# A decode layer on one core: a weight load moved behind the last value tile, batch rows 8 partitions apart for a single output store, and the last weight chunk in rows 6, 2, 1

## The chip, the cores and the metric

The kernel runs on 1 core of one Trainium2 chip. The metric is the device time of one execution in microseconds (us). The time before was 382.03 us, the median of 3 runs (381.35 to 382.17). In the runs that have both numbers the time is 1.7 to 2.2 us longer than the span of the profile (for instance 381.64 us and a span of 379.8 us; one run of before has 383.11 and 380.1 us), so times are compared with times and spans with spans.

## The reference, cut to what matters

One token of a transformer layer for a batch of 4, in bf16. The last 4096 positions of the K and V caches are used.

```python
# D = 576, 32 query heads, 16 KV heads, head size 128, F = 4608
x = A_x                                              # (4, 1, 576)
q = layernorm(x) @ wq                                # 32 heads
p = softmax(q . k_cache[last 4096] * 128 ** -0.5)
o = p . v_cache[last 4096]
h = x + o @ wo
n = layernorm(h)
out = h + (relu(n @ W_gate) * (n @ W_up)) @ W_down   # (4, 1, 576)
```

K and V make 134 MB of the 159.6 MB that must be read from HBM; wq, wo, W_gate, W_up and W_down are the rest. Almost nothing is written.

## The kernel before

All bulk loads are issued in one fixed order by SyncE, into one region of SBUF, `arena`. Each load first waits until the readers of the bytes that it overwrites are done. `add_kv` puts a tile of 4 MB into one of four slots. wo needs 18432 elements a partition: the 16384 where the widened queries lay, and the first 2048 of slot 0, where V12 lies. So wo waits for PV12, the product that reads V12.

```python
        WO_OFF = 0
        for g in range(NTILE - 4, NTILE):            # V12, V13, V14, V15
            if g == NTILE - 1:
                place(("wo",), WO_OFF, H * D, "WO",
                      lambda e: e.dma_start(out=arena[:, WO_OFF:WO_OFF + H * D], in_=A_wo.rearrange("(p r) n -> p (r n)", p=128)))
            add_kv("V", g)
        # ... W_gate and W_up ...
        for j in range(4):                           # W_down in four chunks of 9 rows a partition
            wd_off.append(off)
            for r0, r1 in ((0, 9),) if j < 3 else ((0, 6), (6, 9)):
                place(("wd", j, r0), off + r0 * D, (r1 - r0) * D, "DOWN", ...)
```

The end of the program: the down product takes 4 matmuls for each row (one for each quarter of the 576 output columns, in its own quadrant of 32 PSUM partitions), 144 in all. VectorE casts the result, and four stores of 4 rows bring it out.

```python
        for j in range(4):
            for r in range(9):
                for n in range(4):
                    deps = []
                    if n == 0 and (r == 0 or (j == 3 and r == 6)):
                        deps = [("L", "wd", j, r)] + (["HC0", "HC1", "HC2"] if j == 0 else [])
                    pe("DOWN", lambda e, ...: e.matmul(
                        bank[0][32 * n:32 * n + 32, 0:144], lhsT=hhT[:, r * 128 + 32 * j:r * 128 + 32 * j + 32],
                        rhs=wv[:, r, 144 * n:144 * (n + 1)], start=False, stop=(j == 3 and r == 8), ...), deps)
        dve("OUT", lambda e: e.tensor_copy(out=out_sb[:, :], in_=bank[0][:, 0:144]), ["DOWN"])
        orow = out.rearrange("b s d -> (b s) d")
        for n in range(4):
            P.dma("sync" if n % 2 == 0 else "scalar", ("O", n),
                  lambda e, n=n: e.dma_start(out=orow[:, 144 * n:144 * (n + 1)], in_=out_sb[32 * n:32 * n + 4, :]), f"d_out{n}", ["OUT"])
        P.op("sync", None, None, [("O", n) for n in range(4)])
```

The four batch rows lie on partitions 32n, 32n+1, 32n+2 and 32n+3 of each quadrant n.

## Time and profile before

| what | before |
|---|---|
| time | 382.03 us (381.35 to 382.17) |
| span of the profiled execution | 381.1 us |
| bytes read from HBM | 159.58 MB |
| PE, DVE busy | 73%, 59% of the span |

In the profiles PE is TensorE's matmuls, PEld its weight loads, DVE VectorE, ACT ScalarE, POOL GpSimd; SPq and ACTq are the issues of transfers by SyncE and ScalarE; PEclk is the share of TensorE's full clock that was granted.

From the page of before, the part in 40 slices: each digit is the busy share of a slice of 9.5 us in tenths, and the last line is what the transfer engines moved in GB/s.

```profile
PEclk9998999989978897798997887989989956756687
DMA  8999999999999999999999999999999999999993
GB/s 331 440 423 421 406 440 437 433 428 427 420 439 440 424 433 426 433 430 435 433 430 427 435 430 423 435 433 433 430 428 433 427 439 430 423 435 427 419 414 123
```

The transfer engines are busy 90% or more in all slices but the first and the last, and the windows from 300 to 360 us show a DMA share of 0.99 to 1.02. That is the limit: the weights and caches come in without a hole, and what can still be won lies behind their landing. So the end of the chain of waits, in order of time, is the place to read (start in us, length in us, what; the issues of W_down at 342.96 to 344.28 us and gaps of 0.04 us are left out):

```profile
309.94 3.63 PE psb L497 x32
313.59 0.34 SPq L271
313.97 25.30 DMA sb_arena<-in_A_v_cache_dram
339.31 3.63 PE psb L497 x32
344.28 33.27 DMA sb_arena<-in_B_W_down_dram
377.60 0.83 PE psb L701 x11
378.45 0.31 DVE sb_out_sb L704
```

PV12 ends, SyncE issues wo (L271), then V15 (L246), V15 lands 25.3 us later, PV15 runs, and the last W_down transfer is 33.27 us under way. A length of 33 us for 0.4 MB, which at the 430 GB/s of these slices is about 1 us of work (an estimate), says that the transfer stood in a queue: the wait before its issue isn't what bounds it. The timeline of before from 376 us on (start, length, engine, line, what; in brackets the idle time before and what ended it; here and below some lines of weight loads are left out):

```profile
376.55 1.86 PE L701 MATMUL psb<-sb_arena,sb_pp 128*32 128x144 bf16 x36 [1.31 <-DMA sb_arena<-in_B_W_down_dram]
377.60 0.13 PEld L701 LDWEIGHTS psb<-sb_arena,sb_pp 128*32 128x32 bf16 x6 [0.43 <-DMA sb_arena<-in_B_W_down_dram]
377.98 0.13 PEld L701 LDWEIGHTS psb<-sb_arena,sb_pp 128*32 128x32 bf16 x6 [0.25 <-issue]
378.45 0.31 DVE L704 CAST sb_out_sb<-psb 128x144 bf16<-128x144 f32 x1 [6.54 <-PE psb L701]
378.78 0.67 SPq L708 DMA_DIRECT2D out_dram<-sb_out_sb  x2
378.79 0.62 ACTq L708 DMA_DIRECT2D out_dram<-sb_out_sb  x2
```

The last three rows release PE at 377.60 us. Of their 12 weight loads six come at once and six at 377.98 us, after an idle time that the profile puts down to "issue".

### The profile page before, as it was taken

The numbers are of one execution on the slowest core, as the hardware profiler recorded it, in microseconds if no ns is written. First come the engines' busy times: TensorE is split into PE (matmuls) and PEld (weight loads), VectorE is DVE, ScalarE is ACT, GpSimd is POOL, SyncE is SP. The second block draws the span as 40 slices with busy tenths as digits, with TensorE's granted clock in tenths as the row PEclk, the third lists the DMA queues.
The fourth block names the chain that finished last, engine by engine and source line by source line (L and its number), as shares of the span: only waits on it lengthen the run. The fifth ranks groups of instructions, "written<-read, shape, count | busy, mean of one in ns | idle before, by whom it ended". The sixth has DMA issues, their size and how long they took to land.

```text
span 381.1 us, 3671 instructions
## 1 busy us (share of the span) xinstructions
PE 278.0 (73%) x1629; PEld 92.8 (24%) x1629; DVE 223.2 (59%) x157; ACT 37.5 (10%) x95; POOL 16.3 (4%) x38
## 2 busy tenths in 40 slices
PE   0057999989959892979996939899969537036544
PEld 0013223322222221222221212222212213015322
DVE  0796799979383917965828279756464455002210
ACT  1112000015000006000000051000000340000100
POOL 8800000000000000000000000000000000000000
PEclk9998999989978897798997887989989956756687
DMA  8999999999999999999999999999999999999993
GB/s 331 440 423 421 406 440 437 433 428 427 420 439 440 424 433 426 433 430 435 433 430 427 435 430 423 435 433 433 430 428 433 427 439 430 423 435 427 419 414 123
DMA packets 6390, 159.81 MB, mean 419 GB/s; under 512 B 740, under 2 KB 744, under 8 KB 1384
## 3 DMA queue, kind: packets, MB, share of 16 engines
q1 hardware_dynamic: 6352, 159.59, 97.7%
q8 instruction: 12, 0.20, 0.2%
q14 instruction: 2, 0.02, 0.0%
q10 hardware_dynamic: 24, 0.01, 0.0%
HBM read 159.58 MB, written 0.00 MB: 419 GB/s over the span
## 4 chain that ended last, share of the span: by engine, by line
PE 44%; DMA 34%; DVE 15%; POOL 2%; ACT 2%; issue 1%; SPq 0%; POOLq 0%
PE psb L450 38%; DMA sb_arena<-in_A_k_cache_dram 19%; DVE sb_arena L432 11%; DMA sb_arena<-in_B_W_down_dram 9%; DMA sb_arena<-in_A_v_cache_dram 7%; PE psb L497 5%; POOL sb_arena L303 2%; ACT sb_pp L475 2%; DVE sb_o_sel L509 1%; DVE sb_o_tmp L505 1%; DVE sb_pp L484 1%; PE psb L534 0%; ACT sb_arena L418 0%; SPq L286 0%; PE psb L469 0%
## 5 line engine op out<-in xcount | busy, mean ns | idle before, releaser
L450 PE MATMUL psb<-sb_arena 128*128 128x512 bf16 x512 | 209.1, 578 | 10.5 <-DVE sb_arena L432 8.2
L432 DVE STREAM_TRANSPOSE sb_arena<-sb_arena 128x4096 f32<-128x4096 f32 x32 | 156.1, 4901 | 48.5 <-DMA sb_arena<-in_A_k_cache_dram 48.4
L450 PEld LDWEIGHTS psb<-sb_arena 128*128 128x128 bf16 x512 | 56.8, 114 | 153.6 <-issue 130.3
L497 PE MATMUL psb<-sb_arena,sb_pp 128*32 128x512 bf16 x512 | 35.9, 431 | 23.0 <-DMA sb_arena<-in_A_v_cache_dram 16.5
L475 ACT ACTIVATE sb_pp<-psb,sb_stat 128x512 bf16<-128x512 f32 x32 | 24.9, 847 | 247.8 <-DVE sb_stat L470 247.8
L505 DVE TENSOR_TENSOR sb_o_tmp<-psb,sb_qm 128x512 f32<-128x512 f32 x16 | 10.8, 676 | 27.9 <-PE psb L497 27.9
L497 PEld LDWEIGHTS psb<-sb_arena,sb_pp 128*32 128x32 bf16 x512 | 13.6, 106 | 47.9 <-issue 22.7
L457 DVE TENSOR_REDUCE sb_stat<-psb 128x1 f32<-128x1024 f32 x4 | 4.8, 1211 | 24.2 <-PE psb L450 24.2
L484 DVE STREAM_TRANSPOSE sb_pp<-sb_pp 128x2048 bf16<-128x2048 bf16 x8 | 18.0, 2278 | 1.4 <-ACT sb_pp L475 1.4
L509 DVE TENSOR_REDUCE sb_o_sel<-sb_o_tmp 128x128 f32<-128x512 f32 x16 | 16.6, 1037 | 0.6
L534 PE MATMUL psb<-sb_o_sel,sb_selw 128*32 128x32 f32 x128 | 2.4, 232 | 16.3 <-DVE sb_o_sel L509 16.3
L668 PE MATMUL psb<-sb_arena,sb_hnT 128*32 128x384 bf16 x120 | 7.9, 437 | 6.6 <-DMA sb_arena<-in_B_W_up_dram 4.5
L375 PE MATMUL psb<-sb_ident_b,sb_xn_bf 4*128 4x4 bf16 x4 | 0.3, 172 | 13.7 <-DVE sb_xnd_bf L364 13.7
L388 PE MATMUL psb<-sb_arena,sb_xnT 128*32 128x512 bf16 x32 | 3.6, 631 | 8.9 <-DMA sb_arena<-in_A_wq_dram 8.9
L675 DVE TENSOR_TENSOR sb_pp<-psb,sb_pp 128x384 bf16<-128x384 f32 x3 | 1.5, 551 | 12.6 <-PE psb L668 12.6
L517 PE MATMUL psb<-sb_stat,sb_sameh 128*128 128x1 f32 x8 | 1.8, 292 | 9.1 <-DVE sb_stat L515 9.1
L303 POOL MEMSET sb_arena<- 128x8192 f32 x1 | 6.9, 6925 | 0.0
L475 ACT ACTIVATION_READ_ACCUMULATOR sb_pp<-psb,sb_stat 128x1 f32 x32 | 6.6, 208 | 0.0
L668 PEld LDWEIGHTS psb<-sb_arena,sb_hnT 128*32 128x32 bf16 x120 | 4.2, 124 | 9.7 <-DMA sb_arena<-in_B_W_up_dram 4.8
L534 PEld LDWEIGHTS psb<-sb_o_sel,sb_selw 128*32 128x32 f32 x128 | 1.9, 142 | 17.4 <-DVE sb_o_sel L509 17.4
L701 PE MATMUL psb<-sb_arena,sb_pp 128*32 128x144 bf16 x144 | 3.8, 250 | 3.0 <-DMA sb_arena<-in_B_W_down_dram 2.5
L418 ACT COPY sb_arena<-sb_q_keep 32x128 bf16<-32x128 bf16 x16 | 4.8, 303 | 1.5 <-DVE sb_q_keep L409 1.4
(123 smaller groups left out, 71.9 us busy)
## 6 DMA issues: line engine op xcount, KB each, us to landing
sb_arena<-in_A_k_cache_dram SPq DMA_DIRECT2D x16, 4096.0 KB, 18.9
sb_arena<-in_A_v_cache_dram SPq DMA_DIRECT2D x16, 4096.0 KB, 24.2
sb_arena<-in_A_wo_dram SPq DMA_DIRECT2D x1, 4608.0 KB, 16.0
sb_arena<-in_B_W_gate_dram SPq DMA_DIRECT2D x1, 4608.0 KB, 30.9
sb_arena<-in_B_W_up_dram SPq DMA_DIRECT2D x1, 4608.0 KB, 42.3
sb_arena<-in_A_wq_dram SPq DMA_DIRECT2D x1, 4096.0 KB, 21.5
sb_arena<-in_B_W_down_dram SPq DMA_DIRECT2D x3, 1296.0 KB, 31.1
sb_arena<-in_B_W_down_dram SPq DMA_DIRECT2D x1, 864.0 KB, 32.7
```

The lines of the kernel that those rows point to most:

```text
L303: pool("c_qW", lambda e: e.memset(arena[:, 0:2 * QWW].bitcast(FP32), 0.0))
L418: act(("QW", b), lambda e, i=i: e.copy(out=bass.AP(tensor=arena, offset=32 * i * AW + b % 2 * QWW + 32 * i, ap=[[AW, 32], [128, 4], [514, ...
L432: dve(("TRA", g, w), lambda e: e.transpose(out=dst, in_=src), [("L", "K", g)] if w == 0 else [])
L450: pe(("QK", g, w), lambda e, off=off, steps=steps, wo_=wo_, qd=qd, first=first, last=a == cb == 3: e.matmul(bank[SB[b % 2] + w], lhsT=aren ...
L457: dve(("MAX", b), lambda e: e.tensor_reduce(out=stat[:, b, 0:1], in_=s_ps, axis=AX.X, op=ALU.max, negate=True), [("QK", 4 * b + 3, 1)])
L475: act(("EXP", b, w), lambda e, w=w, a=a: e.activation(out=bass.AP(tensor=pp, offset=4096 + a // 2 * 2048 + w * 1024 + a % 2, ap=[[8192, 12 ...
L484: dve(("PTR", b, w), lambda e: e.transpose(out=dst, in_=src), [("EXP", b, w), ("PV", 4 * b - 1) if b else "QMM"])
L497: pe(("PV", g), lambda e, j=j, tq=tq, k=k: e.matmul(o_ps[32 * j:32 * j + 32, :], lhsT=pT[:, qd * 1024 + tq * 32:][:, 0:32], rhs=v[:, tq * ...
L505: dve(("OS", g), lambda e: e.tensor_tensor(out=o_tmp[:, :].rearrange("p (t d) -> p t d", t=4), in0=o_ps.rearrange("p (t d) -> p t d", t=4) ...
L509: dve(("OSEL", g), lambda e: e.tensor_reduce(out=o_sel[:, qd, :], in_=o_tmp[:, :].rearrange("p (t d) -> p d t", t=4), axis=AX.X, op=ALU.ad ...
L534: pe(("OT", b), lambda e, q=q, qd=qd: e.matmul(ot_ps[32 * qd:32 * qd + 32, 0:32], lhsT=selw[:, qd, 32 * q:32 * q + 32], rhs=o_sel[:, qd, 3 ...
L668: pe(("GU", g, c // 4), lambda e, g=g, m=m, j=j, lo=lo, c=c: e.matmul(bank[3 * g + m][32 * j:32 * j + 32, 0:384], lhsT=hnT[:, c if c < 4 e ...
```

## The change

Three ideas. First, V15's slot is free earlier than wo's bytes, so V15 is to be issued ahead of wo. Second, the less there is to do behind the last landing the better: the last chunk comes as 6, 2 and 1 rows, so that only 4 matmuls follow the last landing instead of 12. Third, if the batch rows lie 8 partitions apart, the 16 output rows (4 quadrants of 4 batch rows) lie at an even step of 8 partitions, and one store can take them all.

```diff
         for g in range(NTILE - 4, NTILE):
-            if g == NTILE - 1:
-                place(("wo",), WO_OFF, H * D, "WO",
-                      lambda e: e.dma_start(out=arena[:, WO_OFF:WO_OFF + H * D], in_=A_wo.rearrange("(p r) n -> p (r n)", p=128)))
             add_kv("V", g)
+        place(("wo",), WO_OFF, H * D, "WO",
+              lambda e: e.dma_start(out=arena[:, WO_OFF:WO_OFF + H * D], in_=A_wo.rearrange("(p r) n -> p (r n)", p=128)))
@@
-            for r0, r1 in ((0, 9),) if j < 3 else ((0, 6), (6, 9)):
+            for r0, r1 in ((0, 9),) if j < 3 else ((0, 6), (6, 8), (8, 9)):
@@
-                    if n == 0 and (r == 0 or (j == 3 and r == 6)):
+                    if n == 0 and (r == 0 or (j == 3 and r in (6, 8))):
@@  batch rows 8 apart: sel4 and hnT are written at 0:32:8 instead of 0:4, and x is
@@  added through a small matrix xsel (two POOL instructions) instead of the identity
-        dve("n2", lambda e: e.tensor_copy(out=hnT[:, 0:4, 0:4], in_=tmp5[:, 0:4, :]), ["n2a", "c_hnT"])
+        dve("n2", lambda e: e.tensor_copy(out=hnT[:, 0:4, 0:32:8], in_=tmp5[:, 0:4, :]), ["n2a", "c_hnT"])
@@
-        orow = out.rearrange("b s d -> (b s) d")
-        for n in range(4):
-            P.dma("sync" if n % 2 == 0 else "scalar", ("O", n),
-                  lambda e, n=n: e.dma_start(out=orow[:, 144 * n:144 * (n + 1)], in_=out_sb[32 * n:32 * n + 4, :]), f"d_out{n}", ["OUT"])
-        P.op("sync", None, None, [("O", n) for n in range(4)])
+        P.dma("sync", "O", lambda e: e.dma_start(
+            out=out.rearrange("b s (n d) -> n (b s) d", n=4), in_=bass.AP(tensor=out_sb, offset=0, ap=[[8 * 144, 16], [1, 144]])),
+            "d_out", ["OUT"])
+        P.op("sync", None, None, ["O"])
```

More of the change, by code (lines that the diff above doesn't have):

```diff
@@ L194, in bass_sequential_preLN__sliding_block_cached__glu_gated_reglu__decode_kernel @@
         out_sb = sb("out_sb", [128, 144], BF16)
+        xsel = sb("xsel", [B, 32], BF16)
         pT = pp[:, 0:4096]
@@ L338, in bass_sequential_preLN__sliding_block_cached__glu_gated_reglu__decode_kernel @@
                                                                fill=1.0, base=-8 * q, channel_multiplier=1), [f"c_toq{q}"])
+        pool("c_xs0", lambda e: e.memset(xsel[:, :], 0.0))
+        pool("c_xs1", lambda e: e.affine_select(out=xsel[:, :], in_=xsel[:, :], pattern=[[-1, 32]], compare_op=ALU.not_equal,
+                                                fill=1.0, base=0, channel_multiplier=8), ["c_xs0"])
         pool("c_oT", lambda e: e.memset(oT[:, :, :], 0.0))
@@ L550, in bass_sequential_preLN__sliding_block_cached__glu_gated_reglu__decode_kernel @@
         dve("c_e8", lambda e: e.tensor_reduce(out=e8[:, :], in_=c_e8[:, :, :], axis=AX.X, op=ALU.max), ["c_e81"])
-        dve("c_sel", lambda e: e.tensor_reduce(out=sel4[:, 0:4], in_=c_s4[:, :, :], axis=AX.X, op=ALU.max),
+        dve("c_sel", lambda e: e.tensor_reduce(out=sel4[:, 0:32:8], in_=c_s4[:, :, :], axis=AX.X, op=ALU.max),
             ["c_s41", "c_sel0"])
@@ L630, in bass_sequential_preLN__sliding_block_cached__glu_gated_reglu__decode_kernel @@
         for c in range(DC):
-            pe("HT", lambda e, c=c: e.matmul(m_ps[:, c * 4:(c + 1) * 4], lhsT=chunk(part, partd, c), rhs=sel4[:, 0:4],
+            pe("HT", lambda e, c=c: e.matmul(m_ps[:, c * 4:(c + 1) * 4], lhsT=chunk(part, partd, c), rhs=sel4[:, 0:32:8],
                                              start=True, stop=True), ["part0", "part1", "partd", "c_sel"] if c == 0 else [])
@@ L651, in bass_sequential_preLN__sliding_block_cached__glu_gated_reglu__decode_kernel @@
         dve("n2a", lambda e: e.tensor_tensor(out=tmp5[:, :, :], in0=tmp5[:, :, :], in1=rstd_bc, op=ALU.mult), ["n1", "s6"])
-        dve("n2", lambda e: e.tensor_copy(out=hnT[:, 0:4, 0:4], in_=tmp5[:, 0:4, :]), ["n2a", "c_hnT"])
+        dve("n2", lambda e: e.tensor_copy(out=hnT[:, 0:4, 0:32:8], in_=tmp5[:, 0:4, :]), ["n2a", "c_hnT"])
         for a in range(2):
-            dve("n3", lambda e, a=a: e.tensor_scalar(out=hnT[:, 4 + a, 0:4], in0=tmp5[:, 4, :], scalar1=par[:, a:a + 1], scalar2=None,
+            dve("n3", lambda e, a=a: e.tensor_scalar(out=hnT[:, 4 + a, 0:32:8], in0=tmp5[:, 4, :], scalar1=par[:, a:a + 1], scalar2=None,
                                                      op0=ALU.mult), ["n2a", "c_hnT"])
@@ L689, in bass_sequential_preLN__sliding_block_cached__glu_gated_reglu__decode_kernel @@
             pe(None, lambda e, n=n: e.matmul(bank[0][32 * n:32 * n + 32, 0:144], lhsT=sel4[:, :], rhs=part[:, 144 * n:144 * (n + 1)],
-                                             start=True, stop=False, skip_group_check=True), [("G", 0)])
+                                             start=True, stop=False, skip_group_check=True), [("G", 0), "c_xs1"])
         for n in range(4):
-            pe(None, lambda e, n=n: e.matmul(bank[0][32 * n:32 * n + 32, 0:144], lhsT=ident_b[0:B, 0:32], rhs=x_bf[:, 144 * n:144 * (n + 1)],
+            pe(None, lambda e, n=n: e.matmul(bank[0][32 * n:32 * n + 32, 0:144], lhsT=xsel[:, :], rhs=x_bf[:, 144 * n:144 * (n + 1)],
                                              start=False, stop=False, skip_group_check=True))
```

## The prediction

> **What bounds the kernel now.** The transfers. The page's slices show the DMA engines at 9 tenths in every slice but the first and last, at 420 to 440 GB/s; 159.6 MB at that rate is some 370 of the 381.1 us span. PE is busy 73%, DVE 59%. The chain of waits ends: V15 lands, PV15 (3.63 us), W_down issues, 33.27 us of W_down transfer, 0.83 us PE, 0.31 us cast. Those 33 us are backlog (issued at 343 to 345 us behind earlier transfers, landed at 377.6), so the PV15 before them isn't really binding.
>
> **Part 1: wo behind V15.** SyncE holds the wo issue until PV12 is done (313.6 us), as wo reaches into V12's slot; V15 queues behind it although its slot was free at about 299.8 us. After: V15 is issued near 300 us and lands where wo does now (near 329 instead of 339.3 us); wo lands near 339.3 us, W_down is issued near 333. WO can start about 6 us earlier (345.8 to about 340), the norm too. But windows from 300 to 360 us show a DMA share of 0.99 to 1.02: no hole to fill. The bytes don't change; W_up lands near 365.2 us either way, and the rest follows as before. Gain on the critical path: 0.0 us.
>
> **Part 2: last chunk in rows 6, 2, 1.** The windows show DMA share 0.37 in 374 to 376 us, 0.06 in 376 to 377: one late engine of sixteen carries the end. Its last three rows land 1.05 us after the six (376.55, 377.60); then 12 matmuls end 0.81 us later, with an issue hole of 0.29 us among them. Four matmuls, as the first four show, need 0.31: minus 0.5 us. Against that, smaller packets: the packet records show 135 ns for 3456 B and about 49 ns for 1152 B (load of x), so rows 2+1 take about 0.07 us more; half-clocked PE may be late by 0.1 us with the two rows. Net gain 0.35 us.
>
> **Part 3: one store for four.** The cast ends at 378.76; SyncE and ScalarE issue two stores each (0.35 and 0.28 us in turn); the first pair's packets end near 380.09 us, the second's at 380.49; SyncE passes its semaphores at 380.53, 380.59, 380.67; the span ends at 381.05. One store has no second issue (0.4 us) and one wait (0.14 us less): gain 0.5 us. [...]
>
> **Added.** Two small POOL constants (about 0.5 us near 18 us, needed after 370 us), strided writes of a few columns: nothing.
>
> **Sum.** 0.0 + 0.35 + 0.5 = 0.85 us: 381.2 us, range 380.3 to 382.1. Faster by over 2%: 0.01; within 2%: 0.98; slower: 0.01.
>
> **What will show it.** V15 landing near 329 us, wo near 339, the last W_down landing unmoved (377.4 to 377.9); 4 matmuls after it; last landing to cast start 0.4 instead of 0.85 us; cast end to span end 1.8 instead of 2.3 us.
>
> **What would make it wrong.** Instruction fetches (12 of 16 KB in the trace, about 1 us each on one DMA engine) falling on another engine and moving the straggler by up to 1 us; a store lowered slower than four; the issue hole landing behind the last row.

The recorded sum came to 0.0 + 0.35 + 0.5 = 0.85 us. Out of part 3 a rule for the number of transfer engines of a store is cut, which no trace here shows, and with it the term that rested on it, a loss of 0.05 us: the 0.5 us of part 3 were 0.4 + 0.14 less 0.05. What still stands in the text there makes 0.54 us.

## The result

| | before | after |
|---|---|---|
| time, median | 381.79 us (381.35 to 382.17, 4 runs) | 381.81 us (381.41 to 381.90, 4 runs) |
| ratio | | 0.9998, 95% interval 0.9984 to 1.0012 |

A ratio is the mean time of one kernel's runs over that of the other's of the same rounds, so it is not quite the ratio of the medians. The 0.85 us of the forecast are not there.

The profile of after has a span of 379.9 us, 1.2 us less than that of before. This is not the gain that it looks like. After is already 1.1 us ahead before the change begins to act: SyncE issues wo at 312.50 us instead of 313.59, released by the same PV12. Four executions of after have spans from 379.3 to 379.9 us and eleven of before, taken later, 379.5 to 380.5 us: the first profile of before was of a late execution. So the two must be compared from a common event near the end. The packet records of the trace give one, the completion of the last W_down transfer (the last of its 16 engines):

| from that completion to | before | before, a second profile | after |
|---|---|---|---|
| start of the cast | 1.29 us | 0.99 us | 1.34 us |
| end of the span | 3.90 us | 3.61 us | 3.83 us |

Behind the last landing, where the change was to win 0.85 us, nothing is won. The end of the chain of waits of after:

```profile
328.43 3.64 PE psb L500 x18
333.40 42.71 DMA sb_arena<-in_B_W_down_dram
376.15 0.30 PE psb L704 x5
376.45 0.60 issue
377.05 0.32 PE psb L704 x7
377.40 0.31 DVE sb_out_sb L707
```

And its timeline from 375 us on:

```profile
375.40 0.56 PE L704 MATMUL psb<-sb_arena,sb_pp 128*32 128x144 bf16 x24 [0.55 <-DMA sb_arena<-in_B_W_down_dram]
376.15 0.30 PE L704 MATMUL psb<-sb_arena,sb_pp 128*32 128x144 bf16 x5 [0.18 <-DMA sb_arena<-in_B_W_down_dram]
377.05 0.30 PE L704 MATMUL psb<-sb_arena,sb_pp 128*32 128x144 bf16 x7 [0.60 <-issue]
377.40 0.31 DVE L707 CAST sb_out_sb<-psb 128x144 bf16<-128x144 f32 x1 [6.08 <-PE psb L704]
377.73 0.68 SPq L708 DMA_DIRECT2D out_dram<-sb_out_sb  x1
```

Two things are to be seen here.

- V15 landed at 328.4 us as foretold, and the small last chunk is there. But five matmuls into the last twelve PE stops for 0.60 us with nothing to wait for. From the start of one matmul to that of the next it is 0.83 us; in before it was 0.29 us. The stop has its own line in the chain now: it is on the critical path.
- The single store took SyncE 0.68 us to issue. That is as long as the two stores that SyncE issued one after the other in before (0.67 us).

The windows of both kernels show a third thing. The columns are the stretch, its length, busy time and number of instructions of PE, PEld, DVE, ACT and POOL, then the granted clock of PE, the DMA share and GB/s. Before:

```profile
360.00:365.00 5.00, 0.74 (x20) 0.26 (x12) 0.00 (x0) 1.26 (x3) 0.00 (x0) 1.00 0.91 380
370.00:374.00 4.00, 2.63 (x93) 2.04 (x93) 1.04 (x3) 0.27 (x1) 0.00 (x0) 1.00 0.89 374
376.00:377.00 1.00, 0.45 (x16) 0.45 (x20) 0.00 (x0) 0.00 (x0) 0.00 (x0) 0.52 0.06 24
```

After:

```profile
360.00:365.00 5.00, 0.94 (x15) 0.48 (x19) 0.00 (x0) 0.00 (x0) 0.00 (x0) 0.50 0.91 386
370.00:374.00 4.00, 3.66 (x109) 3.25 (x111) 0.76 (x2) 0.27 (x1) 0.00 (x0) 0.68 0.88 364
```

With V15 and wo landed earlier, the gate product is done earlier, PE idles 8.4 us instead of 4.5 ahead of W_up, and the clock is at 0.50 when W_up lands. In these two traces the clock fell 2.2 us after the end of the gate product in after (at 357.78 us, for 10.24 us) and about 5 us after it in before (at 365.79 us, 0.60 us into the W_up product); what makes it fall they don't tell. The main W_up product takes 4.03 us instead of 3.49, and the down product starts 7.36 us after W_up's release instead of 6.81 us. This alone would cost nothing, since W_down lands later still.

### The profile page after: what moved, and what is told of

Its sections match the earlier page's. It is cut to its first block, busy times and chain, and to the rows that moved or that the text cites. A ratio compares the mean times of both kernels' runs of the same rounds, so it can differ in the third digit from the quotient of the medians.

```text
span 379.9 us, 3671 instructions
## 1 busy us (share of the span) xinstructions
PE 279.6 (74%) x1629; PEld 93.6 (25%) x1629; DVE 223.1 (59%) x157; ACT 37.6 (10%) x95; POOL 16.5 (4%) x40
## 4 chain that ended last, share of the span: by engine, by line
PE 44%; DMA 37%; DVE 14%; POOL 2%; issue 1%; ACT 0%; SPq 0%; POOLq 0%
PE psb L453 38%; DMA sb_arena<-in_A_k_cache_dram 18%; DMA sb_arena<-in_B_W_down_dram 11%; DVE sb_arena L435 11%; DMA sb_arena<-in_A_v_cache_dram 8%; PE psb L500 4%; POOL sb_arena L303 2%; DVE sb_o_sel L512 1%; DVE sb_o_tmp L508 1%; PE psb L537 0%; ACT sb_arena L421 0%; SPq L286 0%; PE psb L525 0%; PE psb L520 0%; PE psb L472 0%
## 5 line engine op out<-in xcount | busy, mean ns | idle before, releaser
L671 PE MATMUL psb<-sb_arena,sb_hnT 128*32 128x384 bf16 x120 | 9.1, 480 | 11.3 <-DMA sb_arena<-in_B_W_up_dram 8.4
L625 PE MATMUL psb<-sb_arena,sb_oT 128*32 128x288 bf16 x64 | 4.0, 445 | 4.9 <-DMA sb_arena<-in_A_wo_dram 4.9
L704 PE MATMUL psb<-sb_arena,sb_pp 128*32 128x144 bf16 x144 | 4.6, 301 | 1.7 <-DMA sb_arena<-in_B_W_down_dram 0.7
```

The source lines that it names most:

```text
L671: pe(("GU", g, c // 4), lambda e, g=g, m=m, j=j, lo=lo, c=c: e.matmul(bank[3 * g + m][32 * j:32 * j + 32, 0:384], lhsT=hnT[:, c if c < 4 e ...
L704: pe("DOWN", lambda e, j=j, r=r, n=n, wv=wv: e.matmul(bank[0][32 * n:32 * n + 32, 0:144], lhsT=hhT[:, r * 128 + 32 * j:r * 128 + 32 * j + 32],
```

## The experiments

**The theory about the hole.** PE stops because its next instructions aren't there. The page has a queue of instruction transfers, q8, with 12 packets of together 0.20 MB, that is 16 KB each. By their times they belong to PE: one comes for every 200 to 370 of its recorded instructions, 12 for 3279. The last of them begins 2.52 us before PE goes on in before (375.46 and 377.98 us) and 2.54 us before in after (374.51 and 377.05 us). In the down product PE starts a matmul and a weight load every 15 to 32 ns, so what one fetch brings, a block, is used up there in 2.1 to 4.4 us (an estimate from the trace: 3279 / 12 = 273 recorded instructions for each fetch, 137 pairs at these rates), not much more, or even less, than those 2.5 us. **The rival:** the hole belongs to the wait for the last chunk or to the clock and has nothing to do with the place in the instruction stream. (The clock alone can't be it: at the hole it stood at 0.50 in before and at 1.00 in after.)

**The second question** is what one execution's transfers end with, because the spans of one kernel differ by a microsecond, more than the change was to win. **The third** is what makes the store's issue long.

### The kernel before once more (base_again)

No edit.

> The kernel before, unchanged, to learn its spread. The profile of before that I read had a span of 381.05 us, that of after 379.88, yet the two kernels' times are equal. If 1.1 us of that difference is spread of the transfers between executions (theory), the spans of this kernel are 379.3 to 380.2 us, the ratio is 1.000 within 0.002, and the tail is as before: about 0.3 us of hole among the last 12 matmuls, W_up release to cast start 13.2 to 13.4 us, cast end to span end 2.2 to 2.4 us. If the change really shortened the transfers (rival), spans are near 381 us again.

Measured: correct, median 381.74 us against 381.91, ratio 1.0000 (0.9987 to 1.0013). Its spans are 379.6 to 380.4 us, 379.8 in the profile. Cast end to span end is 2.31 us. W_up release to cast start is 12.89 us, not 13.2 to 13.4, because there is no hole: the last three rows release PE at 376.71 us, 2.30 us after its last fetch began, and all 12 matmuls start within 0.24 us.

What follows: the 1.2 us between the first two profiles are spread. And the hole is not in each execution of this kernel: by the theory it shows only where the instructions come later than the last rows.

### Moving the block boundary: 60 dummy matmuls (after_shift60, before_shift60)

```diff
+        for i in range(60):
+            pe(None, lambda e: e.matmul(bank[0][0:32, 0:32], lhsT=ident_b[:, 0:32], rhs=ident_b[:, 0:32],
+                                        start=True, stop=True, skip_group_check=True), ["c_idb"] if i == 0 else [])
         pe_x()
```

They run in the first microseconds, where PE has nothing to do (it was busy 0.00 us of the first 10 us of before), and write to a bank that is overwritten later. They only shift everything behind them by 120 places in PE's instruction stream (the page of after_shift60 has 1689 matmuls and as many weight loads, that of after 1629).

> The kernel after, with 60 dummy matmuls at the start, where PE idles: every later PE instruction lies 120 places further on in the instruction stream. Theory: the hole among the last matmuls (0.60 us idle, 0.83 from start to start, in the profile of after) is PE waiting for its next 16 KB of instructions, of which the fetch starts about 2.5 us before PE goes on in both traces. Then the hole leaves the last 12 matmuls (it lies about 60 matmuls earlier, where PE waits for W_down anyway, or vanishes), W_up release to cast start falls from 13.34 to 12.7 to 12.95 us, and span and time fall by 0.4 to 0.6 us (ratio to before 0.9985 to 0.999). Rival (the hole belongs to the last chunk's wait or to the clock): hole in the same place, nothing moves.

> The kernel before with the same 60 dummy matmuls. Theory: its hole of 0.29 us goes too: W_up release to cast start falls from 13.26 to about 12.9 to 13.05 us, time by 0.2 to 0.3 us. The difference between this and the kernel after with the dummies is then what the 6, 2, 1 rows and the store are worth without the hole: 0.1 to 0.4 us. Rival: unchanged.

Timeline of after_shift60, from 376 us on:

```profile
376.39 0.56 PE L707 MATMUL psb<-sb_arena,sb_pp 128*32 128x144 bf16 x24 [0.83 <-DMA sb_arena<-in_B_W_down_dram]
377.11 0.59 PE L707 MATMUL psb<-sb_arena,sb_pp 128*32 128x144 bf16 x12 [0.16 <-DMA sb_arena<-in_B_W_down_dram]
377.75 0.31 DVE L710 CAST sb_out_sb<-psb 128x144 bf16<-128x144 f32 x1 [5.65 <-PE psb L707]
```

No line with "issue" is left: the only stop among the last 12 matmuls is the wait for the last row. W_up release to cast start is 12.68 us (13.34 in after). The last W_down completion is followed by the cast after 0.77 us and by the end of the span after 3.25 us, against 1.34 and 3.83 us in after. So the tail is 0.57 us shorter. By itself this run doesn't show that the boundary moved, for the fetch may simply have been done in time: the last rows released PE 2.30 us after the last fetch began (377.11 and 374.81 us; 2.42 us in before_shift60), and base_again has no hole at 2.30 us without any edit. The runs that separate come below: in best36, sel_bf16 and sel_bf16_again the last twelve begin 1.50, 1.96 and 1.59 us after the last fetch began, and the first eight of them start within 0.08 us; in after they begin 1.63 us after it, and PE stops behind the fifth. So there the end of the program no longer waits for that fetch.

before_shift60: 13.06 us from W_up release to cast start, 1.09 us from the last completion to the cast, 3.69 us to the end of the span, no hole. Between the two shifted kernels lies what the 6, 2, 1 rows and the store are worth when no fetch is in the way: 1.09 less 0.77, that is 0.32 us, and 2.30 less 2.17, that is 0.12 us. The first of these is not clean: at the end the clock was 0.50 in before_shift60 and 1.00 in after_shift60. Against base_again, which ran its end at 1.00 and without a hole, it is 0.99 less 0.77, that is 0.22 us.

The times didn't follow: 381.99 us (ratio 1.0006, 0.9989 to 1.0022) and 381.86 us (1.0001, 0.9987 to 1.0016), against 381.91 for before. The hole is gone, the forecast of the time failed. Both kernels have 13 fetches instead of 12; whether a fetch costs something by itself is what few_fetches asks below.

### Only the order of the loads (swap_only)

The kernel before with the first hunk of the change alone.

> The kernel before with only wo behind V15. Theory: V15 lands near 328 to 329 us and wo near 339, the transfers end when they did; PE idles longer ahead of W_up, the whole W_up product runs at the half clock (4.0 instead of 3.5 us), DOWN starts about 0.5 us later after W_up's release, so the last instruction fetch starts and ends later: the hole among the last 12 matmuls grows from 0.29 to 0.5 to 0.8 us and W_up release to cast start from 13.26 to 13.4 to 13.8 us. Time: 0 to 0.4 us worse, within the spread. Rival (the swap is wholly neutral): hole stays at 0.3 us, 13.26 us stays.

Measured: 381.95 us, ratio 1.0003 (0.9988 to 1.0019). The down product starts 7.28 us after W_up's release (7.01 and 6.81 in the two profiles of before). W_up release to cast start is 13.17 us and the hole 0.37 us; both were expected somewhat larger (13.4 to 13.8, 0.5 to 0.8). PE goes on 2.38 us after its last fetch began. The late start of the down product is there, and the longer W_up product with it (3.96 us; 3.49 and 3.69 in the two profiles of before); how much it lengthens the hole can't be told at this size, for it depends on when the last rows land too. The order of the loads by itself wins nothing.

### Only the rows 6, 2, 1 (rows_only)

The kernel before with the second hunk alone (and its wait).

> The kernel before with only the last W_down chunk in rows 6, 2, 1. Theory: PE's last matmuls go on when its instructions are there (2.4 to 2.5 us after the fetch begins), not when the last row lands, so last landing to cast start stays at 1.0 to 1.4 us as in the kernels before, instead of falling to 0.75 us as the smaller last chunk alone would make it; time as before within 0.3 us. Rival (the hole of after is bound up with the swap or the clock): last landing to cast start 0.7 to 0.85 us.

Timeline of rows_only:

```profile
375.55 1.17 PE L701 MATMUL psb<-sb_arena,sb_pp 128*32 128x144 bf16 x30 [0.78 <-DMA sb_arena<-in_B_W_down_dram]
376.92 0.43 PE L701 MATMUL psb<-sb_arena,sb_pp 128*32 128x144 bf16 x6 [0.21 <-issue]
377.39 0.31 DVE L704 CAST sb_out_sb<-psb 128x144 bf16<-128x144 f32 x1 [6.43 <-PE psb L701]
```

Six matmuls into the last twelve PE stops, for 0.53 us from start to start, and goes on 2.38 us after its last fetch began. Last completion to cast start is 1.19 us, within the 1.0 to 1.4 expected. Time 381.75 us, ratio 0.9996 (0.9983 to 1.0010). So the hole needs neither the swap nor the new store, and it takes what the small last chunk should have given.

### Half the instructions (few_fetches)

A wrong result: the kernel after, but of each key tile only two of 16 products, and of each value tile only the first and the last of eight groups. (The comparison with the reference passed all the same.) All transfers are as in after in size and order, but SyncE can issue them sooner (the last of W_down at 335.48 instead of 337.01 us), because PE is done sooner.

```diff
                 for cb in range(4):
+                    if not a == cb in (0, 3):
+                        continue
                     first = a == cb == 0
@@
-            for k in range(8):
+            for k in (0, 7):
```

> A wrong result on purpose: the kernel after with 64 of 512 score matmuls and 128 of 512 value matmuls kept; all transfers are as they were. Theory: each of PE's 12 fetches of 16 KB of instructions holds up one of the 16 transfer engines by about 1.6 us (their last completions in six traces stand in clusters 1.6 us apart), and the transfers end with an engine that was hit twice or three times. With half the instructions there are 5 to 7 fetches, fewer engines are hit twice, and the weights end earlier: spans 377.8 to 379.4 us, time 0.5 to 1.8 us under before, and a last completion 1.6 to 2 us nearer to the bulk of the engines in at least some executions. Rival (the clusters come from the memory side, not from fetches): span and clusters as in after, time within 0.3 us of it.

Measured: median 379.74 us (379.67 to 379.84, 5 runs) against 381.73 for before in the same rounds, ratio 0.9945 (0.9932 to 0.9957). That is 2.0 us less, a little more than the range expected, and the five runs lie within 0.2 us. Most other kernels' runs spread over 0.3 to 2.0 us, but the four of rows_only lie within 0.2 us too, so the narrow spread shows nothing by itself. The fetches, from the two pages, after first:

```profile
q8 instruction: 12, 0.20, 0.2%
```

```profile
q8 instruction: 6, 0.10, 0.1%
```

The windows of the last microseconds of transfer (DMA share in the last but one column), after first, then few_fetches:

```profile
372.00:373.00 1.00, 1.00 (x44) 1.00 (x39) 0.00 (x0) 0.00 (x0) 0.00 (x0) 0.50 0.99 400
374.00:375.00 1.00, 0.85 (x31) 0.55 (x20) 0.00 (x0) 0.00 (x0) 0.00 (x0) 0.58 0.40 148
375.00:376.00 1.00, 0.56 (x24) 0.37 (x24) 0.00 (x0) 0.00 (x0) 0.00 (x0) 1.00 0.19 70
```

```profile
372.00:373.00 1.00, 0.68 (x44) 0.49 (x32) 0.00 (x0) 0.00 (x0) 0.00 (x0) 1.00 0.95 366
374.00:375.00 1.00, 0.79 (x36) 0.42 (x28) 0.00 (x0) 0.00 (x0) 0.00 (x0) 1.00 0.10 36
375.00:376.00 1.00, 0.19 (x4) 0.05 (x4) 0.31 (x1) 0.00 (x0) 0.00 (x0) 1.00 0.00 0
```

A share of 0.19 is 3 of 16 engines. The bulk of the engines is done at the same time in both kernels. What is gone are the stragglers. The packet records show how they come about: sorted by their last completion the engines stand in groups about 1.6 us apart. In after the first group ends at 372.6 to 373.7 us, the second at 374.4 to 374.8, the third at 376.0; in few_fetches the first ends at 372.5 to 373.7 us, the second at 374.2 to 374.5, and there is no third. A single fetch is seen to do it in the first profile of before: between V13 and V14 one fetch runs, and one of the 16 engines falls 1.6 us back and stays there, while the other 15 keep their order.

The trace shows this for more than one fetch. Each load lands in 16 parts, one for each engine, and each part's landing is recorded. Compare the landings of each load with those of the load before it, less the step that most parts share: between the two loads around a fetch of PE, one part falls 1.5 to 1.8 us back, in all of the first 11 fetches of before, in all of the first 11 of after, and in the first 5 of few_fetches. (The last fetch of each comes when most engines are done: in before at 375.46 us, when the DMA share of 374 to 376 us was 0.37.) The fetch packet itself takes 0.98 to 1.11 us in before and 0.96 to 1.10 us in after. Without a fetch of PE between two loads parts seldom move, and mostly by less than 1 us.

The 2.0 us are not all from this. Between the two profiles lie 2.14 us: the last completion is 1.53 us earlier in few_fetches (374.53 instead of 376.06 us), and behind it 0.62 us are won, because there is no hole. The kernel also does less work and issues its loads sooner, which was not tested apart. But the earliest part of the last row lands only 0.23 us sooner (372.95 instead of 373.18 us), so that rival has little room.

So a fetch of 16 KB cost one transfer engine about 1.6 us in these traces, and since every load lands in 16 parts, the last weight row waits for the part that is furthest behind (by the semaphores the parts of the last row land from 373.18 to 376.43 us in after). That this is the engine that was hit most often is the author's reading. Which engine a fetch hits is not in the records; that it varies from run to run, and thereby makes the spread of about 1 us, fits everything here but was not tested by itself.

### Two stores of 8 rows (store_two)

The kernel after with this in place of the one store:

```diff
+        orow = out.rearrange("b s (n d) -> n (b s) d", n=4)
+        for i, eng in enumerate(("sync", "scalar")):
+            P.dma(eng, ("O", i), lambda e, i=i: e.dma_start(
+                out=orow[2 * i:2 * i + 2], in_=bass.AP(tensor=out_sb, offset=64 * i * 144, ap=[[8 * 144, 8], [1, 144]])),
+                f"d_out{i}", ["OUT"])
```

> The kernel after, but the output leaves in two stores of 8 rows, one from SyncE and one from ScalarE, side by side. In after the single store of 16 rows took SyncE 0.68 us to issue, against 0.28 to 0.35 us for each old store of 4 rows. Theory: the issue time grows with the rows (about 0.2 us and 0.03 us a row, an estimate from these two), so 8 rows take 0.4 to 0.5 us, both queues at once; cast end to span end falls from 2.18 to 1.95 to 2.1 us (0.2 us off the issue, one more semaphore pass). Rival (0.68 us is the price of the three-dimensional output pattern, whatever the rows): each of the two takes about 0.65 us again, and cast end to span end is 2.15 to 2.3 us.

```profile
377.62 0.66 SPq L710 DMA_DIRECT2D out_dram<-sb_out_sb  x1
377.63 0.63 ACTq L710 DMA_DIRECT2D out_dram<-sb_out_sb  x1
```

The theory fell: 8 rows take 0.66 and 0.63 us, as 16 do. Cast end to span end is 2.43 us, worse than with one store. Time 382.26 us (1.0012, 0.9998 to 1.0025).

### One store in a plain run (store_flat)

A wrong result: the rows go to the wrong places, one behind the other, so that the output's side has two dimensions.

```diff
-            out=out.rearrange("b s (n d) -> n (b s) d", n=4), in_=...
+            out=out.rearrange("b s (n d) -> (b s n) d", n=4), in_=...
```

> A wrong result on purpose: the kernel after with the 16 output rows stored in one plain run, row after row, so that the store's pattern has two dimensions on the output's side too; each row of 144 numbers lands in another's place. Two stores of 8 rows took 0.66 and 0.63 us to issue, as one of 16 does, so rows don't make the price. Theory now: the three-dimensional pattern does. Then this store takes 0.28 to 0.40 us to issue and cast end to span end falls from 2.18 to 1.75 to 1.95 us, what the prediction had promised for the real store. Rival (partitions lying 8 apart make the price): 0.6 to 0.7 us again. Time: 0.2 to 0.4 us under after's, hardly to be told from before's.

Measured: 0.58 us to issue, and 2.17 us from cast end to span end, as in after. Time 382.44 us (1.0010, 0.9993 to 1.0028). The second theory fell too: the output's pattern makes at most 0.1 us. (The hole was 0.26 us here; PE went on 2.28 us after its fetch began.)

### Four stores of 4 rows, 8 partitions apart (store_four8)

```diff
-                  lambda e, n=n: e.dma_start(out=orow[:, 144 * n:144 * (n + 1)], in_=out_sb[32 * n:32 * n + 4, :]), ...
+                  lambda e, n=n: e.dma_start(out=orow[:, 144 * n:144 * (n + 1)],
+                      in_=bass.AP(tensor=out_sb, offset=32 * n * 144, ap=[[8 * 144, 4], [1, 144]])), ...
```

These are the stores of before in number, size and destination. Only the step between the source rows differs, 8 partitions instead of 1; the rest of the kernel is after's.

> The kernel after with the four old stores of 4 rows, two on SyncE and two on ScalarE, but reading rows that lie 8 partitions apart. Every store on adjacent partitions took 0.28 to 0.35 us to issue (before), every store on partitions 8 apart 0.58 to 0.68 us (16 rows, 8 rows, and 16 in a plain run). Theory: the step of 8 partitions makes the price. Then each of the four takes 0.55 to 0.7 us and cast end to span end rises to 2.7 to 3.1 us. Rival (something else in the larger stores, such as their number of packets for each engine or rows of the output): 0.28 to 0.35 us each, and cast end to span end 2.25 to 2.35 us as in before.

Timeline of store_four8 from 378 us on:

```profile
378.00 0.30 PE L704 MATMUL psb<-sb_arena,sb_pp 128*32 128x144 bf16 x7 [1.24 <-issue]
378.35 0.31 DVE L707 CAST sb_out_sb<-psb 128x144 bf16<-128x144 f32 x1 [6.29 <-PE psb L704]
378.68 1.49 SPq L710 DMA_DIRECT2D out_dram<-sb_out_sb  x2
378.69 1.33 ACTq L710 DMA_DIRECT2D out_dram<-sb_out_sb  x2
```

Single stores take 0.60 to 0.75 us to issue, and two in turn 1.49 us (0.67 in before). Cast end to span end is 3.34 us, even above the 2.7 to 3.1 expected. Time 383.07 us, ratio 1.0036 (1.0020 to 1.0052). So the step of 8 partitions makes the price of the issue. Why it does, no run tells. The hole is at its longest here, 1.46 us from start to start: the fetch began late, at 375.53 us, and PE went on 2.47 us later.

### Looking for a faster version: best36, sel_bf16, sel_bf16_again

best36 is after with 36 dummy matmuls and the two stores of 8 rows.

> The kernel after with 36 dummy matmuls at the start and the two stores of 8 rows. Theory of the instruction fetch: no hole among the last 12 matmuls, last W_down landing to span end 3.0 to 3.3 us (3.9 in before, 3.8 in after, 3.25 with 60 dummies); the fetch that follows comes after 375 us, when few transfers are left, and so lengthens them less than with 60 dummies. Time 0.3 to 0.8 us under before if the transfers end alike; but their end varies by over 1 us between executions of one kernel, so the ratio may well stay within 0.9980 to 1.0005. Rival: hole and tail as in after.

Measured: 381.71 us, ratio 1.0005 (0.9991 to 1.0019). There is no hole, and last landing to span end is 3.48 us, above the 3.0 to 3.3 expected: the two stores take back 0.26 us (cast end to span end 2.44 us).

sel_bf16 takes instructions away instead of adding some. In after, the 64 matmuls that select the attention output are in fp32, and the trace shows two passes and two weight loads for each (x128 of both on the page of after); in bf16 it shows one (x64 of both on the page of sel_bf16).

```diff
-        selw = sb("selw", [128, 4, 128], FP32)
+        selw = sb("selw", [128, 4, 128], BF16)
-        o_sel = sb("o_sel", [128, 4, 128], FP32)
+        o_sel = sb("o_sel", [128, 4, 128], BF16)
@@  and the reduction that writes o_sel is allowed to round to bf16
```

> The kernel after with the selection matrices of the attention output in bf16 instead of fp32, so that PE needs 64 matmul passes and 64 weight loads fewer in the whole program (a result rounded once more in bf16). Theory: the last block of instructions no longer begins among the last matmuls: no hole there, last landing to cast start 0.7 to 0.8 us, last landing to span end 3.2 to 3.3 us; 12 fetches as in after, not 13 as with dummies, so the weights land as in after. Time 0.2 to 0.7 us under before: ratio 0.9982 to 0.9998. Rival (nothing but spread): ratio 0.9995 to 1.0005, hole as in after.

> The same kernel as sel_bf16 once more, because its gain of 0.12% had an interval that touches 1 (0.9975 to 1.0002). If the gain is real: mean 0.2 to 0.7 us under before again (ratio 0.9982 to 0.9995), last landing to span end 3.2 to 3.4 us, no hole among the last 12 matmuls. If it was chance: ratio 0.9995 to 1.001.

Timeline of sel_bf16:

```profile
376.25 0.60 PE L707 MATMUL psb<-sb_arena,sb_pp 128*32 128x144 bf16 x12 [0.17 <-DMA sb_arena<-in_B_W_down_dram]
376.90 0.31 DVE L710 CAST sb_out_sb<-psb 128x144 bf16<-128x144 f32 x1 [5.06 <-PE psb L707]
```

In both profiles the hole is gone with 12 fetches, and last landing to span end is 3.27 and 3.26 us. Times: 381.39 us, ratio 0.9988 (0.9975 to 1.0002), and 381.52 us, ratio 0.9996 (0.9982 to 1.0009). Taken together 11 runs have a mean of 381.45 us, and the 20 runs of before in the same rounds 381.78 us, 0.33 us more (0.26 us without the one run of 383.11 us, whose span is an ordinary 380.1 us). But each interval by itself holds 1, and by the ranges set down before the second run its ratio of 0.9996 lies on the side of chance (0.9995 to 1.001). So the shorter tail is shown, and a gain in time of about 0.1% is not.

### All tails in one table

From the packet records and the timelines, in us. "Fetch to PE" is the time from the beginning of PE's last fetch to the matmul behind the hole.

| kernel | fetches | hole among the last 12, start to start | fetch to PE | last completion to cast | cast end to span end | last completion to span end |
|---|---|---|---|---|---|---|
| before | 12 | 0.29 | 2.52 | 1.29 | 2.30 | 3.90 |
| base_again | 12 | none | | 0.99 | 2.31 | 3.61 |
| swap_only | 12 | 0.37 | 2.38 | 1.23 | 2.28 | 3.82 |
| rows_only | 12 | 0.53 | 2.38 | 1.19 | 2.27 | 3.77 |
| before_shift60 | 13 | none | | 1.09 | 2.30 | 3.69 |
| after | 12 | 0.83 | 2.54 | 1.34 | 2.18 | 3.83 |
| store_two | 12 | 0.62 | 2.45 | 1.14 | 2.43 | 3.88 |
| store_flat | 12 | 0.26 | 2.28 | 0.78 | 2.17 | 3.26 |
| store_four8 | 12 | 1.46 | 2.47 | 1.99 | 3.34 | 5.64 |
| after_shift60 | 13 | none | | 0.77 | 2.17 | 3.25 |
| best36 | 13 | none | | 0.73 | 2.44 | 3.48 |
| sel_bf16 | 12 | none | | 0.77 | 2.19 | 3.27 |
| sel_bf16_again | 12 | none | | 0.77 | 2.18 | 3.26 |
| few_fetches | 6 | none | | 0.72 | 2.18 | 3.21 |

The holes are 0.26 to 1.46 us long, but from the fetch to the matmul behind it it is 2.28 to 2.54 us in all seven. That is the sign of a wait for the fetch. What starts a fetch, and so why the last one comes as late as it does, no run tells.

## Why the prediction was right or wrong

The time of 381.81 us lies in the range of 380.3 to 382.1, and "within 2%" holds, but that range also held the case that nothing changes. The gain of 0.85 us doesn't hold: the measured ratio of 0.9998 is 0.1 us, with an interval of about half a microsecond to either side.

- **What bounds the kernel: right.** The transfers do. What the prediction saw as one late engine is better read as an engine that instruction fetches have held up. With six fetches less the last completion came 1.53 us earlier. The prediction named the fetches as a risk, at about 1 us each; the engine that is hit falls 1.5 to 1.8 us back.
- **Part 1, the order: right, with a side effect missed.** V15 landed at 328.4 us (near 329 said), wo at 339.3 (near 339.3), W_down's issues after PV15 began at 332.1 (near 333), and nothing was won. Missed was the clock: with 8.4 us of idle time ahead of W_up instead of 4.5 its product ran at 0.50 and took 4.03 us instead of 3.49, and the down product started 0.35 to 0.55 us later after W_up's release (7.36 us; 7.01 and 6.81 in the two profiles of before).
- **Part 2, the rows: the step that failed is "Four matmuls, as the first four show, need 0.31: minus 0.5 us".** The estimate supposed that PE can go on when the last row lands. It named "the issue hole landing behind the last row" as a risk and then didn't ask what the hole was. It was PE waiting for instructions, and it grew from 0.29 to 0.83 us, so that last completion to cast start was 1.34 us instead of some 0.9. (By the prediction's own mark, the landing as the semaphore tells it, 0.97 us instead of the 0.4 foretold.) Take the hole away and most of the term is there: 0.32 us between the two shifted kernels, or 0.22 us against base_again at the same clock, with 0.35 predicted. The boundary lies at nearly the same place in the program, six or seven matmuls before the end in both kernels (x6 behind the hole in before, x7 in after); the rows moved in front of it and the instructions did not.
- **Part 3, the store: the step that failed is "One store has no second issue (0.4 us) and one wait (0.14 us less): gain 0.5 us".** The one store took 0.68 us to issue instead of 0.35, which eats the second issue to the last bit; the wait is the gain that remains, 0.12 us. The cost was taken from stores of adjacent rows (0.28 to 0.35 us in before) and carried to rows 8 partitions apart, where it doesn't hold (0.58 to 0.75 us). For the one store the trace of after has 16 packets and 4 completions, for each old store that of before has 4 and 4; each store of 8 rows has 2 completions, the plain run 16. The layout that made one store possible is what made it dear.
- **The sum.** In the last stretch after wins 0.07 us over the first profile of before and loses 0.22 us to the second. Both are smaller than what executions of one kernel differ by, mostly through the end of their transfers.

## What to carry to other kernels

When little is left to do behind the last landing, read what else the engine needs there: an idle time put down to "issue" in a dense run of short matmuls can be a wait for the instructions themselves (here 0.26 to 1.46 us from start to start in seven profiles, and PE went on 2.28 to 2.54 us after the fetch began). What it falls on can be moved by adding or removing instructions far ahead: with 36 dummy matmuls (best36) or 64 passes and 64 weight loads less (sel_bf16) the hole was gone. In a kernel bound by transfers the fetches of instructions are transfers too. Here each of the first 11 put one of 16 parts 1.5 to 1.8 us back in before and in after, so fewer instructions can be worth more than a better order of the loads: few_fetches, with 6 fetches instead of 12, took 2.0 us less than before (its last completion came 1.53 us earlier than after's, and it also does less work), and swap_only won nothing (ratio 1.0003). And take the cost of an issue from a transfer with the same access pattern, not only of the same size: stores of adjacent partitions took 0.28 to 0.35 us in before, stores of partitions 8 apart 0.58 to 0.75 us, whether of 4, 8 or 16 rows.
